# Masks of a small softmax: two full-array matmuls ahead of the scores, or twelve 32-column ones behind them

## The chip, the cores and the metric

The kernel runs on one core of one Trainium2 chip. The metric is the device time in microseconds of one execution, the median over several. The core has a matrix engine (TensorE, PE in the profile, its weight loads PEld), VectorE (DVE), ScalarE (ACT), GpSimd (POOL) and SyncE (SP), which issues most DMAs.

## The reference

The whole program is four layers, A B A B, each added to the residual stream `x` of 2048 tokens of width 640. The change concerns layer B, a recurrent memory transformer with 32 heads of width 128:

```python
mask = (idx[:, None] < M) | (idx[:, None] >= idx[None, :])   # M = 8, L = 40
for s in range(n_seg):                                       # 64 segments of 32 tokens
    h = jnp.concatenate([mem, xs], axis=1)                   # 8 + 32 rows
    q, k, v = (jnp.einsum('btd,dhe->bhte', h, W) for W in (Wq, Wk, Wv))
    scores = jnp.einsum('bhqe,bhke->bhqk', q, k) * scale
    scores = jnp.where(mask[None, None], scores, -1000000000.0)
    p = _softmax(scores, axis=-1)
    o = jnp.einsum('bhqk,bhke->bhqe', p, v)
    o = jnp.einsum('bhte,hed->btd', o, Wo)
    mem = o[:, :M, :].copy()
    outs.append(o[:, M:, :])
```

The eight memory rows see everything; the other 32 rows are causal. The memory of one segment comes out of the segment before, so the 64 steps of a layer form a chain.

## The kernel before, in words

Layer B (`layer_B`) runs 64 steps, twice in the program, 128 in all. The order of the instructions on TensorE, ScalarE, VectorE and GpSimd is the order in which the code issues them: every engine is wrapped in `_OrdNC`, which chains each instruction behind the one before on its engine. All profile lines of layer B read L101, the line of that wrapper, so groups are told apart by tile names.

A step `s` projects 32 columns, the 8 memory rows and the first 24 tokens of a segment, with 32-column tiles of the matrix engine, four side by side: K and Q for heads 0 to 15 (`b_Ka`, `b_Qa`) and for heads 16 to 31 (`b_Kb`, `b_Qb`). Each result is evacuated from PSUM to a bf16 tile `b_kq`, by ScalarE for Ka, Kb and Qb and by VectorE for Qa, and transposed back with four full-array matmuls (`transp4`: `b_TPak`, `b_TPaq`, `b_TPbk`, `b_TPbq`). VectorE copies the memory rows of each transpose into `QT[s]` and `KT[s]`, and ScalarE the 24 token rows into those of step `s + 1`.

The last 8 tokens of each segment (the tails) do not depend on the memory. They are projected for eight segments at a time in spare places of the chain (`tail_unit`, tile `b_tail`), go through DRAM, and are copied by GpSimd (`tails_copy`) into `KT[s]` and `QZ[s % 2]`. `QZ` holds the tail queries of head pairs: 8 columns of the even head, zeros, 8 columns of the odd head.

The scores are built in two PSUM tiles of rows of 40 keys. `SPa` has 8 such rows per partition: 4 for the tail queries and 4 for the 32 other queries of heads 0 to 15; `SPb` has 4, for heads 16 to 31. `mask_mm` writes the masks first, as identity times `mask12` over the full 128x128 array: 320 columns into `SPa` between the transposes `b_TPbk` and `b_TPbq`, and 160 into `SPb` behind `b_TPbq`. `scores` then adds 64 matmuls of 40 columns in 32-column tiles: 16 with `b_QT` (heads 0 to 15), 32 with `b_QZ` (16 weight columns each) and 16 with `b_QT` (heads 16 to 31).

`mask12` is zero outside a few columns: in the tail rows only keys 0 to 7 are masked anywhere, in the other rows only keys 0 to 31 (the order of keys in `KT` is tail, tokens, memory).

The softmax follows: negated row maxima (`b_negmax`) and their addition to `SPa` and `SPb` on VectorE, the exponential (`b_E`) on ScalarE, sums (`b_ssum`), reciprocals and the products `b_Px` on VectorE and `b_Pm` on GpSimd. Meanwhile TensorE does the V projections (`b_Va`, `b_Vb`) and 30 matmuls of `b_tail`. Then it transposes the probabilities (`p_transp`, tile `b_PTP`), does 10 more of `b_tail`, the products with V (`b_OTP`), the output projection (`b_OPS`, and `b_OPSd` for the tails of earlier steps), and extracts the new memory (`b_MT`), with which the next step's K and Q begin.

Most PSUM tiles of layer B rotate through five buffers (`ps_tile`); `b_tail` and `b_TPbq` share one of their own.

Of the kernel before, what the change touches and what calls it, by code (L numbers as in the profile page):

```python
# [18 lines left out]
F32 = mybir.dt.float32  # L19
BF16 = mybir.dt.bfloat16  # L20
# [521 lines left out]
def layer_B(nc, tc, C, W, x_src, xb_src, x_dst, mem0, B_Wv, B_Wo, nsteps=64, out_bf16=False, tag=""):  # L542
    SCB = 1.0 / math.sqrt(128.0)
    nc_raw = nc
    nc = _OrdNC(tc, nc_raw, engines=ORDER_ENGINES)
# [4 lines left out]
    with ExitStack() as ctx:  # L550
        def pool(name, bufs):
            return ctx.enter_context(tc.tile_pool(name=name, bufs=bufs, reuse_waits="tile"))
# [8 lines left out]
        st = pool("b_state", 1)  # L561
# [10 lines left out]
        def ps_tile(shape, dtype, name):  # L572
            return pp.tile(shape, dtype, name=name, tag="ps")
# [2 lines left out]
        Px = st.tile([128, 12, 32], BF16, name="b_Px")  # L576
        Pm = st.tile([128, 12, 32], BF16, name="b_Pm")
        mask12 = st.tile([128, 12, 40], BF16, name="b_mask12")
        QZ = [st.tile([128, 16, 24], BF16, name=f"b_QZ{i}") for i in range(2)]
        selm = st.tile([128, 2, 8], BF16, name="b_sel")  # L580
        HXz = st.tile([128, NCH, 1, 32], BF16, name="b_HXz")
        OTdef = [wk.tile([128, 32, 32], BF16, name=f"b_OTdef{i}") for i in range(2)]
# [1 line left out]
        def init_state():  # L584
# [7 lines left out]
            for i in range(2):  # L592
                nc.gpsimd.memset(QZ[i][:], 0.0)
            negs = wk.tile([128, 32], F32, name="b_negs", tag="PTa")
# [71 lines left out]
        def transp4(sb, name, tp=None):  # L666
            if tp is None:
                tp = ps_tile([128, 4, 128], BF16, name)
            for i in range(4):
                nc.tensor.transpose(tp[:, i, :], sb[:, 128 * i:128 * i + 128], C.identb[:])  # L670
            return tp
# [10 lines left out]
        def tails_load(s):  # L682
            tl = bx.tile([128, 2, 32, 8], BF16, name="b_tl", tag="tl")
            nc.sync.dma_start(tl[:].rearrange("p a h t -> p (a h t)"), QKd[s])
            return tl

        def tails_copy(s, tl):
            for e in range(2):
                nc.gpsimd.tensor_copy(QZ[s % 2][:, :, 16 * e:16 * e + 8], tl[:, 0, :, :].rearrange("p (x e) t -> p e x t", e=2)[:, e])
            nc.gpsimd.tensor_copy(KT[s][:, :, 0:8], tl[:, 1, :, :])  # L690

        def vtails_in(s):
# [96 lines left out]
        for (nm, b), sb in zip(jobs, sbs):  # L789
            tp = transp4(sb, "b_TP")  # L790
            scatter("dve" if nm == "K" else "act", tp, b, KT[0] if nm == "K" else QT[0], 8, 32, 8 if nm == "K" else 0)
        XO, XOd = init_state()
        tails_copy(0, tails_load(0))
        Vth = VH[-1] = w2.tile([128, 2, 512], BF16, name="b_Vth", tag="Vth")
        for k in range(8):
# [61 lines left out]
        for s in range(nsteps):  # L857
# [7 lines left out]
            if not last:  # L865
                alloc_seg(s + 1)
                tl = tails_load(s + 1)
# [3 lines left out]
            def x_scatter(tp, b, D_):  # L871
                if not last:
                    scatter("act", tp, b, D_[s + 1], 8, 32, 8 if D_ is KT else 0)
# [5 lines left out]

            GR = ((0, 8), (8, 12))  # L880

            def mask_mm(a):
                g0, g1 = GR[a]
                SP = ps_tile([128, g1 - g0, 40], F32, f"b_SP{a}")
                nc.tensor.matmul(SP[:].rearrange("p g k -> p (g k)"), lhsT=C.identb[:], rhs=mask12[:, g0:g1, :].rearrange("p g k -> p (g k)"),
                                 start=True, stop=False, skip_group_check=True)
                return SP

            def scores(SPs):
                for b in range(2):  # L890
                    for j in range(4):
                        for i in range(4):
                            h = 16 * b + 4 * j + i
                            nc.tensor.matmul(SPs[b][32 * i:32 * i + 32, j + 4 * (1 - b), :], lhsT=QT[s][:, h, :], rhs=KT[s][:, h, :],
                                             start=False, stop=True, tile_position=(0, 32 * i), skip_group_check=True)
                    if b == 0:
                        qz = QZ[s % 2][:].rearrange("p x c -> p (x c)")
                        for j in range(4):
                            for e in range(2):
                                for t4 in range(4):  # L900
                                    pr = 8 * (t4 // 2) + 2 * j + t4 % 2
                                    nc.tensor.matmul(SPs[0][32 * t4:32 * t4 + 16, j, :], lhsT=qz[:, 24 * pr + 8 * e:24 * pr + 8 * e + 16],
                                                     rhs=KT[s][:, 2 * pr + e, :],
                                                     start=False, stop=True, tile_position=(0, 32 * t4), skip_group_check=True)

            negmax = sm.tile([128, 12], F32, name="b_negmax", tag="negmax")
            ssum = sm.tile([128, 12], F32, name="b_ssum", tag="ssum")
# [2 lines left out]

            def soft_max(a, SP):
                nc.vector.tensor_reduce(out=negmax[:, slice(*GR[a])], in_=SP[:], axis=AX.X, op=ALU.max, negate=True)

            def soft_sub(a, SP):
                n_ = GR[a][1] - GR[a][0]
                nc.vector.tensor_tensor(out=SP[:], in0=SP[:], in1=negmax[:, slice(*GR[a])].unsqueeze(2).to_broadcast([128, n_, 40]), op=ALU.add)

# [45 lines left out]
            TPbk = transp4(kb, "b_TPbk")  # L963
            scatter("dve", TPbk, 1, KT[s], 0, 8, 32)
            x_scatter(TPbk, 1, KT)
            SPa = mask_mm(0)
            TPbq = transp4(qb, "b_TPbq", po.tile([128, 4, 128], BF16, name="b_TPbq", tag="tail"))
            scatter("dve", TPbq, 1, QT[s], 0, 8, 24)
            x_scatter(TPbq, 1, QT)
            SPb = mask_mm(1)  # L970
            scores((SPa, SPb))
            soft_max(0, SPa)
            soft_max(1, SPb)
# [10 lines left out]
            if not last:  # L984
                tails_copy(s + 1, tl)
# [55 lines left out]
            if not last:  # L1041
# [5 lines left out]
                for pi, (ca, cb) in enumerate(parts):  # L1047
                    mt = ps_tile([128, cb - ca, 8], F32, f"b_MT{pi}")
                    for c in range(ca, cb):
                        for q in range(4):  # L1050
                            o = 64 * c + 32 * (q % 2)
                            nc.tensor.matmul(mt[32 * q:32 * q + 32, c - ca, :], lhsT=msb[:, o:o + 32], rhs=selm[:, q // 2, :],
                                             start=True, stop=True, tile_position=(0, 32 * q), skip_group_check=True)
# [22 lines left out]
def full_kernel(tc, A_x, A_wq, A_wk, A_wv, A_wo, A_beta, B_x, B_mem0, B_Wq, B_Wk, B_Wv, B_Wo, B_seg_len, out, layers="ABAB"):  # L1076
    nc = tc.nc
    with ExitStack() as ctx:
# [15 lines left out]
        for li, L in enumerate(layers):  # L1094
            lastl = (li == nl - 1)
            if L == "A":
                first = li == 0

                def side(G, after):
                    load_B_resident(nc, WB, B_Wq, B_Wk, G, after)  # L1100
                    if G == 6:
                        keep_padded(nc, tc, WA, padded)

                layer_A(nc, tc, C, WA, xin if first else X, X, first, xb_dst=Xb,
                        load_w=lambda: load_A_weights(nc, WA, A_wq, A_wk, A_wv, A_wo, padded, stage),
                        side_loads=(side, A_beta) if first else None)
            else:
                layer_B(nc, tc, C, WB, X, Xb, xout if lastl else X, mem0, B_Wv, B_Wo, out_bf16=lastl, tag=str(li))
# [58 lines left out]
```

## Time and profile before

| what | value |
|---|---|
| median of 3 runs | 2805.99 us (2799.53 to 2806.8) |
| profiled execution | 2809.46 us, its span 2807.7 us |
| mean granted clock of TensorE | 0.984 |
| TensorE matmul busy | 2637.4 us, 94% of the span, 65416 records |
| TensorE weight loads busy | 1720.3 us, 61% |
| VectorE busy | 1688.6 us, 60% |
| ScalarE busy | 1589.9 us, 57% |
| mask matmuls of `b_SP` | 128 of 320 columns, mean 299 ns, and 128 of 160 columns, mean 233 ns |
| score matmuls with `b_QT` | 4096, mean 185 ns |
| score matmuls with `b_QZ` | 4096, mean 181 ns |

How to read it: a step of layer B takes some 14.9 us, so 128 steps make two thirds of the time. Matmuls are drawn from their start to a modelled end and overlap each other, so a mean of 185 ns says little of what one costs: what counts is how far apart the starts of neighbours are. Weight loads run beside matmuls.

### The profile page before, as it was taken

To read this page: it belongs to the slowest core of one execution; us is meant where nothing else is said; L and a number is where in the kernel's file an instruction comes from. 1 tells how busy PE (TensorE), PEld (TensorE's weight loads), DVE (VectorE), ACT (ScalarE), POOL (GpSimd) and SP (SyncE) were. 2 spreads that over 40 slices of the span, in tenths; PEclk is the share of its full clock that TensorE was granted. 3 is DMA by queue.
4 is the path that set the end of the run, shared out by engine and by line. 5 is a ranking of instruction groups with operands and counts; after the bars stand their busy time and mean duration, and the time that the engine had idled before them with its cause. 6 is when DMAs were issued, how large, how long until landed. Compare 5 with 4: busy or idle time off the path is not lost.

```text
span 2807.7 us, 146964 instructions
## 1 busy us (share of the span) xinstructions
PE 2637.4 (94%) x65416; PEld 1720.3 (61%) x65480; DVE 1688.6 (60%) x4553; ACT 1589.9 (57%) x3708; POOL 701.5 (25%) x1645
## 2 busy tenths in 40 slices
PE   5899988999999999999979999899999999999998
PEld 3555555666666666666645555556666666666665
DVE  6788864555555555545568888545555555555554
ACT  3778864555555555544448888445555555455443
POOL 3566651111111111111135666411111111111110
PEclk9999989999999999999989999899999999999999
DMA  6110143122122122111130111621111121111110
GB/s 213 65 44 30 30 165 104 41 45 45 41 44 44 41 47 46 39 42 31 29 112 21 58 48 37 218 55 40 42 41 39 42 43 40 42 41 36 39 27 20
DMA packets 322302, 156.36 MB, mean 56 GB/s; under 512 B 245761, under 2 KB 310401, under 8 KB 318593
## 3 DMA queue, kind: packets, MB, share of 16 engines
q1 hardware_dynamic: 320224, 136.47, 19.2%
q8 instruction: 512, 8.39, 1.3%
q10 hardware_dynamic: 1440, 10.49, 1.1%
q14 instruction: 126, 1.02, 0.1%
HBM read 95.15 MB, written 51.71 MB: 52 GB/s over the span
## 4 chain that ended last, share of the span: by engine, by line
PE 76%; ACT 8%; DVE 8%; issue 3%; DMA 3%; POOL 2%; SPq 0%; ACTq 0%; POOLq 0%; DVEq 0%
PE b_OPS L101 10%; PE b_tail L101 6%; PE b_Ka L101 5%; PE b_Qb L101 5%; PE b_Kb L101 5%; PE b_Qa L101 5%; PE b_Va L101 5%; PE b_Vb L101 5%; PE b_SP L101 4%; PE b_OTP L101 3%; DVE a_nm L369 3%; ACT a_PT L404 3%; PE b_PTP L101 3%; PE b_OPSd L101 3%; PE b_vtail L101 3%
## 5 line engine op out<-in xcount | busy, mean ns | idle before, releaser
L101 PEld LDWEIGHTS <-b_HX 128*32 128x32 bf16 x15360 | 435.9, 97 | 337.2 <-issue 15.8
L369 DVE TENSOR_REDUCE a_nm<-a_S 128x2 f32<-128x1024 f32 (+3 forms) x512 | 403.1, 808 | 70.0 <-PE a_T L401 58.1
L101 POOL TENSOR_TENSOR b_Pm<-b_E,b_rs 128x96 bf16<-128x96 bf16 x128 | 63.4, 495 | 1446.2 <-ACT b_Vth L101 1118.7
L404 ACT ACTIVATE a_PT<-a_T 128x1024 bf16<-128x1024 f32 (+1 forms) x384 | 342.3, 895 | 77.9 <-PE a_T L401 72.7
L101 PE MATMUL b_OPS<-b_wo,b_OTsb 128*32 128x320 bf16 x8192 | 309.7, 301 | 12.2 <-issue 9.9
L101 PEld LDWEIGHTS <-b_OTsb 128*32 128x32 bf16 x8192 | 202.1, 97 | 96.4 <-DVE b_OTsb L101 24.1
L406 POOL TENSOR_SCALAR_AFFINE_SELECT a_PT<-a_PT 128x256 bf16<-128x256 bf16 (+1 forms) x384 | 204.4, 534 | 196.1 <-ACT a_PT L404 195.4
L101 DVE CAST b_HX<-b_MT 128x8 bf16<-128x8 f32 x372 | 63.7, 172 | 280.4 <-PE b_MT L101 275.2
L101 ACT CAST b_msb<-b_OPS 128x64 bf16<-128x64 f32 x378 | 69.6, 257 | 239.5 <-PE b_OPS L101 239.5
L101 ACT CAST b_kq<-b_Kb 128x512 bf16<-128x512 f32 x128 | 74.9, 585 | 201.4 <-PE b_Kb L101 201.4
L101 DVE COPY b_KT<-b_TPak 128x128 bf16<-128x128 bf16 x128 | 28.8, 225 | 226.7 <-PE b_TPak L101 226.7
L101 PE MATMUL b_Va<-b_wv,b_HX 128*32 128x512 bf16 x2520 | 161.0, 380 | 0.0
L101 PE MATMUL b_Vb<-b_wv,b_HX 128*32 128x512 bf16 x2520 | 160.2, 379 | 0.0
L101 PEld LDWEIGHTS <-b_kq 128*128 128x128 bf16 x2080 | 116.8, 98 | 69.4 <-ACT b_kq L101 55.2
L101 PE MATMUL b_Ka<-b_wk,b_HX 128*32 128x512 bf16 x2520 | 159.3, 379 | 0.0
L101 PE MATMUL b_Qb<-b_wq,b_HX 128*32 128x512 bf16 x2520 | 159.2, 379 | 0.0
L101 PE MATMUL b_Kb<-b_wk,b_HX 128*32 128x512 bf16 x2520 | 159.2, 379 | 0.0
L101 PE MATMUL b_Qa<-b_wq,b_HX 128*32 128x512 bf16 x2520 | 159.2, 379 | 0.0
L101 DVE TENSOR_SCALAR b_kq<-b_Qa 128x512 bf16<-128x512 f32 x128 | 88.6, 692 | 116.7 <-PE b_Qa L101 113.7
L401 PE MATMUL a_T<-a_q,a_kT 32*128 32x512 bf16 (+3 forms) x1024 | 137.4, 305 | 19.5 <-DVE a_nm L369 12.9
L101 DVE CAST b_OTsb<-b_OTP 128x160 bf16<-128x160 f32 (+1 forms) x384 | 122.3, 374 | 39.3 <-PE b_OTP L101 39.3
L101 PE MATMUL b_vtail<-b_wv,b_TX 128*32 128x256 bf16 x2880 | 138.0, 271 | 7.9 <-issue 4.9
(195 smaller groups left out, 5777.3 us busy)
## 6 DMA issues: line engine op xcount, KB each, us to landing
b_QKd<-b_tu SPq DMA_DIRECT2D x128, 128.0 KB
b_tl<-b_QKd SPq DMA_DIRECT2D x128, 128.0 KB
b_wv<-in_B_Wv_dram SPq DMA_DIRECT2D x10, 1024.0 KB
b_wo<-in_B_Wo_dram SPq DMA_DIRECT2D x16, 640.0 KB
b_VTd<-b_vt SPq DMA_DIRECT2D x256, 32.0 KB
b_Vth<-b_VTd SPq DMA_DIRECT2D x512, 16.0 KB
b_XO<-xres SPq DMA_DIRECT2D x256, 30.0 KB
b_wk<-in_B_Wk_dram ACTq DMA_DIRECT2D x5, 1024.0 KB
```

Of the source, the lines that this page charges most:

```text
L101: r = f(*a, **k)
L369: nc.vector.tensor_reduce(out=nm[:, qc, 2 * pr:2 * pr + 2], in_=X[:, :, o:o + w_], axis=AX.X, op=ALU.max, negate=True)
L401: nc.tensor.matmul(Y[:, e, o:o + w_], lhsT=kT[rows, 128 * kc:128 * kc + 128], rhs=q2[rows, 128 * kc:512], start=True, stop=True, tile_posi ...
L404: nc.scalar.activation(out=PT[:, :, b:b + width], in_=Y[:, :, 0:width], func=ACT.Exp, scale=SC)
L406: nc.gpsimd.affine_select(out=dv, in_=dv, pattern=[[0, 2], [0, diag], [1, 128]], compare_op=ALU.is_ge, fill=0.0, base=0, channel_multiplie ...
```

## The change

`mask_mm` no longer opens the PSUM tiles. The first score matmul of each tile and quadrant does that (`start=(j == 0)`), and the masks are added behind the scores, in 32-column tiles of the array (weights: 32 columns of the identity), only in the columns where `mask12` is not zero: for `SPa` four matmuls of 4 x 8 columns (tail rows) and four of 4 x 32, for `SPb` four of 4 x 32. `SPb`'s masks stand behind its own scores.

The tail queries' matmuls wrote 16 of each 32 partitions; the other 16 were covered by the mask matmul. Now the matmul of the even head writes 32: `QZ` has 40 columns per head pair instead of 24, with 24 zeros in the middle.

```diff
-        QZ = [st.tile([128, 16, 24], BF16, name=f"b_QZ{i}") for i in range(2)]
+        QZ = [st.tile([128, 16, 40], BF16, name=f"b_QZ{i}") for i in range(2)]
...
-                nc.gpsimd.tensor_copy(QZ[s % 2][:, :, 16 * e:16 * e + 8], tl[:, 0, :, :].rearrange("p (x e) t -> p e x t", e=2)[:, e])
+                nc.gpsimd.tensor_copy(QZ[s % 2][:, :, 32 * e:32 * e + 8], tl[:, 0, :, :].rearrange("p (x e) t -> p e x t", e=2)[:, e])
...
-            def mask_mm(a):
+            def sp_tile(a):
                 g0, g1 = GR[a]
-                SP = ps_tile([128, g1 - g0, 40], F32, f"b_SP{a}")
-                nc.tensor.matmul(SP[:].rearrange("p g k -> p (g k)"), lhsT=C.identb[:], rhs=mask12[:, g0:g1, :].rearrange("p g k -> p (g k)"),
-                                 start=True, stop=False, skip_group_check=True)
-                return SP
+                return ps_tile([128, g1 - g0, 40], F32, f"b_SP{a}")
+
+            def mask_mm(SP, o0, o1, m0, w_):
+                for k in range(4):
+                    nc.tensor.matmul(SP[32 * k:32 * k + 32, o0:o1, 0:w_], lhsT=C.identb[:, 32 * k:32 * k + 32],
+                                     rhs=mask12[:, m0:m0 + o1 - o0, 0:w_],
+                                     start=False, stop=True, tile_position=(0, 32 * k), skip_group_check=True)
...
                             nc.tensor.matmul(SPs[b][32 * i:32 * i + 32, j + 4 * (1 - b), :], lhsT=QT[s][:, h, :], rhs=KT[s][:, h, :],
-                                             start=False, stop=True, tile_position=(0, 32 * i), skip_group_check=True)
+                                             start=(j == 0), stop=False, tile_position=(0, 32 * i), skip_group_check=True)
...
-                                    nc.tensor.matmul(SPs[0][32 * t4:32 * t4 + 16, j, :], lhsT=qz[:, 24 * pr + 8 * e:24 * pr + 8 * e + 16],
+                                    m_ = 16 if e else 32
+                                    nc.tensor.matmul(SPs[0][32 * t4:32 * t4 + m_, j, :], lhsT=qz[:, 40 * pr + 24 * e:40 * pr + 24 * e + m_],
                                                      rhs=KT[s][:, 2 * pr + e, :],
-                                                     start=False, stop=True, tile_position=(0, 32 * t4), skip_group_check=True)
+                                                     start=False, stop=False, tile_position=(0, 32 * t4), skip_group_check=True)
+                        mask_mm(SPs[0], 0, 4, 0, 8)
+                        mask_mm(SPs[0], 4, 8, 4, 32)
+                mask_mm(SPs[1], 0, 4, 4, 32)
...
-            SPa = mask_mm(0)
+            SPa = sp_tile(0)
             TPbq = transp4(qb, "b_TPbq", po.tile([128, 4, 128], BF16, name="b_TPbq", tag="tail"))
             scatter("dve", TPbq, 1, QT[s], 0, 8, 24)
             x_scatter(TPbq, 1, QT)
-            SPb = mask_mm(1)
+            SPb = sp_tile(1)
             scores((SPa, SPb))
```

## The prediction

> **What bounds the kernel now.** I read the profile page first, then the timeline of one B step, then the waits. The page's chain of waits is almost all TensorE:
>
> ```profile
> PE 76%; ACT 8%; DVE 8%; issue 3%; DMA 3%; POOL 2%; SPq 0%; ACTq 0%; POOLq 0%; DVEq 0%
> ```
>
> That share invites the reading "fewer matmul columns, less time". It is an average over unlike places, so I looked at the two spots where the change acts. The first is the timeline of one step from the last Q projection to the softmax (start, length, engine, operation):
>
> ```profile
> 1007.85 0.60 ACT L101 ACTIVATE b_kq<-b_Qb 128x512 bf16<-128x512 f32 x1 [0.50 <-PE b_Qb L101]
> ...
> 1008.29 0.10 PEld L101 LDWEIGHTS <-c_identb 128*128 128x128 bf16 x1
> ...
> 1008.35 0.30 PE L101 MATMUL b_SP<-b_mask,c_identb 128*128 128x320 bf16 x1
> ...
> 1008.50 0.23 PEld L101 LDWEIGHTS <-b_kq 128*128 128x128 bf16 x4
> ...
> 1008.73 0.23 PE L101 MATMUL b_SP<-b_mask,c_identb 128*128 128x160 bf16 x1
> ...
> 1008.90 0.28 PE L101 MATMUL b_SP<-b_KT,b_QT 128*32 128x40 bf16 x16
> ...
> 1009.01 0.41 PE L101 MATMUL b_SP<-b_KT,b_QZ 128*16 128x40 bf16 x32
> ...
> 1009.25 0.32 PE L101 MATMUL b_SP<-b_KT,b_QT 128*32 128x40 bf16 x16
> ...
> 1009.52 0.72 DVE L101 TENSOR_REDUCE b_negmax<-b_SP 128x8 f32<-128x320 f32 x2 [0.36 <-PE b_SP L101]
> ```
>
> Two things are to be seen. ScalarE's evacuation of Qb ends at 1007.848 + 0.597 = 1008.445, and the weight load for `b_TPbq` starts at 1008.496. In all 128 steps of the two B layers that load starts 50 to 52 ns after that evacuation ends: the four transposes wait for ScalarE, and the first mask matmul (148 ns from its start to theirs) stands inside this wait. And VectorE is idle until the scores of `SPa` are complete.
>
> The second spot is the next meeting of VectorE and TensorE, on the weight loads before `b_PTP`:
>
> ```profile
> 1012.32 0.27 PEld L101 LDWEIGHTS <-b_wk 128*128 128x128 bf16 x7
> 1012.72 0.11 PEld L101 LDWEIGHTS <-b_Px 128*128 128x128 bf16 x2
> 1012.92 0.11 PEld L101 LDWEIGHTS <-b_Pm 128*128 128x128 bf16 x2
> 1013.07 0.11 PEld L101 LDWEIGHTS <-b_Px 128*128 128x128 bf16 x2
> ```
>
> VectorE's two `b_Px` products end at 1012.662 and 1013.018, and the loads that need them start 54 ns later; the second distance is 52 to 54 ns in all 128 steps. TensorE has nothing to do at 1012.55, when the last of the thirty `b_tail` matmuls has streamed. The matmul rows hide this, since each is drawn some 180 ns or more long. So the cycle that sets a step is: Qb, its evacuation, `b_TPbq`, scores of `SPa`, softmax on VectorE and ScalarE, `b_PTP`. TensorE's work between `SPa` and `b_PTP` has slack.
>
> **The change part by part.** Nanoseconds per step, from the starts of single matmuls in this step; the spread over the steps is a few ns where none is given.
>
> *First mask matmul removed: 0.* Its cover is the evacuation. Without it `b_TPbq` could start 56 ns after the last `b_TPbk` matmul instead of 56 + 148, but the load still waits until 1008.496. If that were not a real wait, 148 ns would come free (a rival).
>
> *Second mask matmul removed: −67.* It stands between the last `b_TPbq` matmul and the first score, with no wait that ends later: 56 ns to it, then 163 to the scores. 163 is 67 for 160 columns (2.4 columns per ns, the pace at which 512-column matmuls in four tiles follow each other, 54 ns apart) plus 96 for going from the full array to 32-column tiles. That step stays: elsewhere it is 126 after 27 ns of columns (`b_tail` to `b_OTP`) and 152 after 53 (layer A). So 53 + 98 = 151 replaces 219. The scores' own inputs are ready: `b_QT` from `b_TPaq` ends at 1008.550, and the scores would start at 1008.83; the second half needs `b_QT` from `b_TPbq`, ending at 1009.158 plus 51, and would start at about 1009.27.
>
> *A separate semaphore instruction before the first score: 0.* In the built program the score's load now carries two waits, for the buffer's last writer (Kb, long past) and VectorE. Such an instruction already stands in the `b_tail` to `b_OTP` turn, which costs 99 beyond its columns, no more than turns without one.
>
> *Weight tiles of the tail queries 32 instead of 16 wide (16 of 32): 0.* The loads last 93 and 86 ns, but lie beside matmuls: rounds of four matmuls start every 25 ns both with `b_QT` (32 wide) and with `b_QZ` (16 wide).
> The Trainium skill, "TensorE: Matmul & The Clock Gate", section "LDWEIGHTS (loading the stationary operand)", makes a load cost its columns ÷ 1.2 ns, 13 ns more for each widened one; over four tiles side by side that would be an estimated 53 ns per step, 6.8 us in all. The equal rounds of 25 ns speak against paying it, since in them the load is hidden.
>
> *Eight mask matmuls ahead of `SPa`'s release: +104.* From about the 33rd score on, pairs of load and matmul start 8.3 ns apart, so eight add 67. The last one streams 128 columns where the last `b_QZ` streams 40: 88 ÷ 2.4 = 37 more before it is done. Writing runs of 8 or 32 into rows of 40 costs nothing extra: `b_PTP` does exactly that and its matmuls follow each other at 55 ns for 128 columns and 26 to 28 for 32, like contiguous ones.
>
> *Release of VectorE.* From the last `b_QZ` start to `b_negmax` it now takes 277; 314 with the longer matmul. The other bound is the nearest 128-column row, `b_TPbq` to its VectorE copy: 255. I take 314, because the same kind of matmul in the same place gives it; 255 would make the sum −22 instead of +37.
>
> *Second-half masks, +53, and the later start of Va: 0.* TensorE reaches `b_PTP` about −67 + 33 + 53 + 53 = 72 later, `b_PTP` itself waits 37 longer; in the step shown it waits 164 at the first load and longer in all. `SPb` is ready about 100 later than now, and VectorE takes it up only 0.41 us after `SPa`.
>
> *POOL and SP:* same instructions; two memsets per layer grow from 384 to 640 elements, in the prologue. The copies into `QZ` keep their size and count.
>
> Sum: −67 + 67 + 37 = **+37 ns per step, times 128 = +4.7 us**, 2814.2 us against the profiled execution (2809.46, its span 2807.7 plus 1.8) and **2810.7** against the median of 2805.99, which lies 3.5 below that execution; the shown runs spread over 7.3. With the 255 ns bound: −22 × 128 = −2.8, 2803.2. 0.3% is 8.4 us, about what a measurement of this kernel can tell from no change; both ends lie inside it.
>
> **The rivals.**
>
> *The dense run breaks up more often (slower).* In 57 of the 128 steps `b_negmax` starts later than the usual 277, by 128 ns on average and up to some 220, 7.3 us in all. In most of them TensorE's starts also show one hole among the last of the 64 scores, never before the 57th pair. No wait explains it; it looks as if a long run of such short instructions outruns something. The run grows from 64 to 76 pairs, and `SPa` completes after the 56th instead of the 48th. If every step lost the mean of 128, 71 more would cost 9.1 us: +13.8, **2819.8**; with 220 in each step +25.5, 2831.5. Against it: some late steps show no hole, so length need not be the cause. It decides over no change from about 29 more late steps (3.7 us).
>
> *`b_TPbq` moves up (faster).* If the load at 1008.496 only stood behind the 320 columns (133 ns), the step would gain 148 more: 37 − 148 = −111, −14.2 us, **2791.8**. For: 148 is not far above 133. Against: the constant 50 to 52 ns to the evacuation's end, while the distance to the mask matmul varies from 135 to 153.
>
> *Wide loads are paid.* If each of the 16 held up the row difference of 7 ns in a single file, 112 ns on the chain: +149 in all, 19.1 us, **2825.1**. The rounds of 25 ns speak against it. The skill's rule above is a milder form of this and would give 2817.5, within this rival's chance.
>
> *TensorE takes over before `b_PTP`.* If the slack is smaller than the profile shows, +72 counts instead of +37: 9.2 us, **2815.2**. It decides where the waits on `b_Px` vanish; the 52 to 54 ns in every step speak against it.
>
> *The change doesn't do what it says* is unlikely: the built order has 12 mask matmuls behind the scores and none ahead.
>
> **How the numbers follow.** Forecast with both bounds: 0.60, between 2803 and 2811 plus a few us of spread. Dense run: 0.22. `b_TPbq` moves up: 0.10. Wide loads: 0.04. TensorE takes over: 0.04. Faster by over 0.3%: 0.10, from the second rival alone. Slower by over 0.3%: 0.22 + 0.04 + 0.04 = 0.30. Within: 0.60. The range runs from 2798, the lower bound less the spread of runs, to 2824, which takes in most of the dense run's cases; outside are the second rival, the wide loads in single file and every step at 220.
>
> **What would show it.** Right: `b_TPbq` loads still 50 to 52 ns after the Qb evacuation; 151 ns from the last `b_TPbq` matmul to the first score; mask matmuls 8.3 ns apart; `b_negmax` some 314 after the last of them; `b_PTP` still 53 after `b_Px`. Wrong: the load earlier than the evacuation allows, scores in rounds longer than 33 ns, holes ahead of `SPa`'s last mask matmul, or more late `b_negmax` than 57.

## The result, and the profile after

The changed kernel takes **2824.77 us** (median of 6 runs, 2818.03 to 2827.35) beside 2804.94 for the kernel before (6 runs, 2799.53 to 2807.38): ratio 1.0073, 95% interval 1.0062 to 1.0084. It is slower by 19.8 us. The forecast was 2810.7, less than 0.3% above before, and its range ended at 2824: the result lies just above it. The profiled execution of the change took 2827.12 us, its span 2825.4 at a clock of 0.982; against the profiled one of before (2807.7) that is 17.7 us of span to explain.

First the place of the change. The timeline of one undisturbed step after it (start, length, engine, operation; the idle time before it and who ended that in brackets):

```profile
1029.47 0.60 ACT L101 ACTIVATE b_kq<-b_Qb 128x512 bf16<-128x512 f32 x1 [0.50 <-PE b_Qb L101]
...
1030.12 0.23 PEld L101 LDWEIGHTS <-b_kq 128*128 128x128 bf16 x4 [0.16 <-ACT b_kq L101]
1030.12 0.40 PE L101 MATMUL b_TPbq<-c_identb,b_kq 128*128 128x128 bf16 x4
...
1030.45 0.28 PE L101 MATMUL b_SP<-b_KT,b_QT 128*32 128x40 bf16 x16
...
1030.56 0.41 PE L101 MATMUL b_SP<-b_KT,b_QZ 128*32 128x40 bf16 x32
...
1030.80 0.28 PE L101 MATMUL b_SP<-b_mask,c_identb 128*32 128x32 bf16 x8
...
1030.90 0.29 PE L101 MATMUL b_SP<-b_KT,b_QT 128*32 128x40 bf16 x16
...
1031.01 0.25 PE L101 MATMUL b_SP<-b_mask,c_identb 128*32 128x128 bf16 x4
...
1031.14 0.72 DVE L101 TENSOR_REDUCE b_negmax<-b_SP 128x8 f32<-128x320 f32 x2 [0.35 <-PE b_SP L101]
```

Both full-array masks are gone, `b_TPbq` is still released by ScalarE's evacuation, and the twelve small masks stand where the diff puts them. From the start of `b_TPbq` to `b_negmax` it is 1017 ns here, and 1017 in such a step of before (15th percentile over the steps; 1016 after). So in an undisturbed step the change moves the chain by nothing. But fewer steps are undisturbed: `b_negmax` comes more than 30 ns later than this in 52 of the 128 steps before and in 68 after. The rest of the loss lies further down.

At the second meeting, before `b_PTP`, nothing has changed either. In the step ahead of the one shown VectorE's products end at 1018.33 + 0.78 = 1019.11, and the load that needs the second starts right behind that:

```profile
1018.33 0.78 DVE L101 TENSOR_TENSOR b_Px<-b_E,b_rs 128x256 bf16<-128x256 bf16 x2
...
1018.81 0.11 PEld L101 LDWEIGHTS <-b_Px 128*128 128x128 bf16 x2
...
1019.17 0.11 PEld L101 LDWEIGHTS <-b_Px 128*128 128x128 bf16 x2
```

The page's chain of waits doesn't tell the difference: it is TensorE as before, one per cent more.

```profile
PE 77%; ACT 8%; DVE 7%; issue 3%; DMA 2%; POOL 1%; SPq 0%; ACTq 0%; DVEq 0%; POOLq 0%
```

The waits of TensorE that nothing in the profile releases ("issue": waited in us, times, longest us), first before, then after:

```profile
PE b_OPS L101 <- issue: 9.9, 18, 1.0
...
PE b_vtail L101 <- issue: 4.9, 10, 0.7
PE b_OPSd L101 <- issue: 4.2, 5, 1.2
PE b_MT L101 <- issue: 4.1, 10, 0.9
```

```profile
PE b_OPS L101 <- issue: 16.2, 25, 1.5
...
PE b_OPSd L101 <- issue: 7.3, 7, 4.0
...
PE b_vtail L101 <- issue: 6.5, 13, 0.9
```

These are idle times of TensorE inside the output projection, which begins some 5.5 us behind the masks, and they grow. The timeline of one such place after, and the same stretch of another step without a hole:

```profile
714.62 1.53 PE L101 MATMUL b_OPS<-b_wo,b_OTsb 128*32 128x320 bf16 x40
...
717.66 0.46 PE L101 MATMUL b_OPS<-b_wo,b_OTsb 128*32 128x320 bf16 x8 [1.51 <-issue]
...
718.22 0.55 ACT L101 CAST b_msb<-b_OPS 128x64 bf16<-128x64 f32 x3 [3.47 <-PE b_OPS L101]
```

```profile
730.43 2.36 PE L101 MATMUL b_OPS<-b_wo,b_OTsb 128*32 128x320 bf16 x64
```

64 matmuls take 2.36 us when they run through; here the last 8 start 1.5 us late with their inputs long ready, and ScalarE's `b_msb`, the new memory, waits behind them. This is on the chain of every step: `b_msb`, `b_MT`, `b_HX`, the next `b_Ka`.

Where does the 17.7 us go? Means over 126 steps, from the starts of single instructions, in ns:

| stretch of the step | before | after | difference |
|---|---|---|---|
| start of `b_TPbq` to `b_negmax` | 1074 | 1099 | +25 |
| `b_negmax` to the last `b_PTP` | 3713 | 3721 | +8 |
| first to last `b_OPS` (median 2058, 2059) | 2186 | 2293 | +106 |
| all else | 8054 | 8059 | +5 |
| whole step | 15027 | 15172 | +145 |

145 × 126 = 18.3 us, the whole loss. 106 of it are the holes in `b_OPS`; 25 come from the steps in which `b_negmax` is late. The undisturbed value of neither stretch moves.

**What the holes are.** The program has 131104 TensorE instructions before and 133792 after, and the page lists a queue that carries TensorE's instructions (packets, MB, share of the DMA engines), before and after:

```profile
q8 instruction: 512, 8.39, 1.3%
```

```profile
q8 instruction: 522, 8.55, 1.3%
```

131104 ÷ 512 = 256.06 and 133792 ÷ 522 = 256.3: a packet is a block of 256 instructions. Counted from the program's start, the first instruction behind a hole is nearly always number 194 or 195 of its block: 66 of the 86 holes over 0.35 us from `b_OPS` to `b_MT` after, 48 of 69 before, and no other number more than twice. The one above is number 25795 = 100 × 256 + 195. TensorE had started the load before it at 715.842, a packet landed at 716.080, and TensorE went on at 717.663. I read that as some 62 instructions taken in ahead of time, so that what is late is the next block. In those 66 holes (48 before) the median from the landing to the next start is 1.40 us (1.43). The packet takes 1.13 us on average, and in layer B it starts 1.04 us (median; 0.93 before) after TensorE has come within 64 instructions of the end of the block two before. By this reading it takes some 3.5 us (the sum of the three) from there until the new block can be used, so TensorE must stop when it uses up 256 instructions in less; no two packets start less than 3.29 us apart. From the first `b_OTP` load on, 256 instructions are used up in 2.84 us (medians). And from the first score to the start of the last `b_OPS` matmul an undisturbed step takes 7.85 us with 577 instructions before, and 7.91 us with 601 after: 3.48 and 3.37 us per block, just about as fast as blocks come.

The Trainium skill, "Runtime: NRT & Kernel Launch", section "Instruction fetch mechanics", has the blocks of 256 instructions, which agrees, but gives TensorE room for 2048 instructions and says that the fetch is hidden, because dispatch is slower than the fill. This trace disagrees: in 94 steps of equal length the holes at block edges sum to 31.4 us before and 50.0 after.

### The profile page after: what moved, and what is told of

Its sections match the earlier page's. It is cut to its first block, busy times and chain, and to the rows that moved or that the text cites. A ratio compares the mean times of both kernels' runs of the same rounds, so it can differ in the third digit from the quotient of the medians.

```text
span 2825.4 us, 149652 instructions
## 1 busy us (share of the span) xinstructions
PE 2652.7 (94%) x66696; PEld 1723.8 (61%) x66760; DVE 1688.6 (60%) x4553; ACT 1595.3 (56%) x3708; POOL 702.4 (25%) x1645
## 3 DMA queue, kind: packets, MB, share of 16 engines
q14 instruction: 125, 1.02, 0.1%
## 4 chain that ended last, share of the span: by engine, by line
PE 77%; ACT 8%; DVE 7%; issue 3%; DMA 2%; POOL 1%; SPq 0%; ACTq 0%; DVEq 0%; POOLq 0%
PE b_OPS L101 10%; PE b_tail L101 6%; PE b_Ka L101 5%; PE b_Kb L101 5%; PE b_Qb L101 5%; PE b_Qa L101 5%; PE b_Va L101 5%; PE b_Vb L101 5%; PE b_SP L101 4%; PE b_OTP L101 3%; ACT a_PT L404 3%; DVE a_nm L369 3%; PE b_vtail L101 3%; PE b_OPSd L101 3%; PE b_PTP L101 3%
## 5 line engine op out<-in xcount | busy, mean ns | idle before, releaser
L101 PE MATMUL b_OPS<-b_wo,b_OTsb 128*32 128x320 bf16 x8192 | 315.6, 301 | 19.6 <-issue 16.2
L401 PE MATMUL a_T<-a_q,a_kT 32*128 32x512 bf16 (+3 forms) x1024 | 138.0, 306 | 16.9 <-DVE a_nm L369 10.4
```

Of the source, the lines that this page charges most:

```text
L101: r = f(*a, **k)
L401: nc.tensor.matmul(Y[:, e, o:o + w_], lhsT=kT[rows, 128 * kc:128 * kc + 128], rhs=q2[rows, 128 * kc:512], start=True, stop=True, tile_posi ...
```

## The experiments

The theories: **supply**, the number of TensorE instructions per step sets the loss, wherever they stand; **late release**, the masks behind the scores delay `b_negmax` in more steps (the first rival of the prediction); **chain**, the eight masks cost their length ahead of the release. All kernels were timed beside the kernel before on the same chip; "late" is the sum by which steps go over the kernel's own usual time from `b_TPbq` to `b_negmax` by more than 30 ns; "holes" is the excess at block edges in the 94 equal steps. Late and holes come from one profiled execution each. Before was traced once, so its 7.1 and 31.4 stand beside traces from other chips.

| kernel | instr. per step | ratio to before [95%] | late, us | holes, us |
|---|---|---|---|---|
| before | 869 | 1 | 7.1 | 31.4 |
| after | 890 | 1.0073 [1.0062, 1.0084] | 10.4 | 50.0 |
| after_again | 890 | 1.0052 [1.0040, 1.0064] | 9.5 | 34.1 |
| after_c | 890 | 1.0054 [1.0040, 1.0068] | 8.7 | 47.1 |
| after_d | 890 | 1.0045 [1.0030, 1.0060] | 9.8 | 31.1 |
| pad10 | 889 | 1.0012 [1.0002, 1.0021] | 6.5 | 27.6 |
| pad10_b | 889 | 1.0010 [0.9999, 1.0022] | 5.9 | 33.5 |
| pad10_scores | 889 | 1.0026 [1.0016, 1.0035] | 7.1 | 30.5 |
| pad15 | 899 | 1.0032 [1.0020, 1.0044] | 6.6 | 25.9 |
| pad20 | 909 | 1.0073 [1.0060, 1.0086] | 6.2 | 42.9 |
| long4 | 877 | 1.0026 [1.0017, 1.0036] | 5.9 | 24.1 |
| before_less10 | 849 | 0.9988 [0.9976, 1.0000] | 5.0 | 26.2 |
| before_less10_b | 849 | 0.9983 [0.9970, 0.9996] | 5.3 | 25.7 |
| after_less10 | 870 | 1.0021 [1.0010, 1.0031] | 9.0 | 31.7 |
| after_less20 | 850 | 1.0014 [1.0005, 1.0022] | 9.3 | 23.4 |
| spa_unmasked | 890 | 1.0032 [1.0020, 1.0044] | 8.1 | 38.9 |
| masks_ahead | 871 | 0.9985 [0.9974, 0.9995] | 6.9 | 22.8 |
| masks_ahead_less10 | 851 | 0.9960 [0.9947, 0.9974] | 6.9 | 32.8 |

The same changed kernel shows 31 to 50 us of holes on different chips, so a single trace tells where the holes are, and only the ratios what a kernel costs.

**More instructions, away from the scores.** Pairs of weight load and 8-column matmul ahead of `b_Va`, where TensorE has slack; and four pairs of 512 columns, many columns in few instructions:

```diff
-        def thin_mm(cols_ap, Wt, b, name):
+        def thin_mm(cols_ap, Wt, b, name, pad=0, pad_w=8):
             ps = ps_tile([128, 512], F32, name)
+            for k in range(pad):
+                j = k % 4
+                nc.tensor.matmul(ps[32 * j:32 * j + 32, 0:pad_w], lhsT=cols_ap[:, 0, :], rhs=Wt[:, 0, 512 * (4 * b + j):512 * (4 * b + j) + pad_w],
+                                 start=True, stop=True, tile_position=(0, 32 * j), skip_group_check=True)
...
-            Va = thin_mm(cols, W.wv, 0, "b_Va")
+            Va = thin_mm(cols, W.wv, 0, "b_Va", pad=10, pad_w=8)   # pad15: 15, pad20: 20, long4: pad=4, pad_w=512
```

pad10: 

> The kernel before, with ten extra pairs of weight load and 8-column matmul per step, written into Va's PSUM tile ahead of its real first matmul, which overwrites them. Theory S (supply): TensorE's instructions reach it in blocks of 256, and from the scores to the output projection a step uses them about as fast as they come, so an instruction added there costs 5.7 ns although TensorE has slack at that place: 20 x 5.7 x 126 steps = +14 us, as holes without a wait in b_OPS; bounds +5 and +33 (13.3 ns each, the shortest distance of two blocks over 256). Theory D (dense scores and a longer mask chain): nothing in this kernel touches scores or masks, 0. Theory L (TensorE late at b_PTP): 83 ns of TensorE time in the slack, 0 if the slack holds, +10 at most.

pad20: 

> The kernel before with twenty pairs in Va's tile, twice as many as in pad10 (which gave +3.5 us). S: the more instructions a block's worth of time has to hold, the more edges stall: +7 us if linear, up to +20. L (TensorE late at b_PTP): 166 ns of TensorE time, 0 to +5, since 213 ns with few instructions gave +7.

pad15: 

> The kernel before with fifteen such pairs ahead of Va, 899 instructions a step. Ten cost 3 us, twenty 20. If the supply has a knee just above the count of pad10 and the change, fifteen cost 10 to 15 us; if the cost grows only well past the change's count, 5 us or less.

long4: 

> The kernel before, with four extra pairs of 512 columns at the same place: 213 ns more TensorE time in the slack ahead of b_PTP, but 8 instructions instead of 20. S: +5.7 us, bounds 0 and +13. L: if later V projections are what costs, 213 ns is nearly three times the 72 of the change, +27 us. D: 0.

pad10_b, beside the change on one chip: 

> The ten pairs in Va's tile again, now on the same chip as the changed kernel. S: as many instructions per step as the change (889 against 890), none of them on the chain: +4 to +12 us over the kernel before, and the changed kernel some 3 us (its late b_negmax) above that. If the masks' place matters beyond that, the changed kernel stays 10 us above this one.

Ten pairs cost 3.4 to 3.5 us (2801.34 beside 2797.82, 2807.55 beside 2804.16), fifteen 8.0 (2801.80 beside 2793.77), twenty 20.2 (2814.91 beside 2794.67), on four chips in all. So instructions that do nothing cost time in a place with slack, by these runs more than in proportion, and twenty of these pairs cost as much as the whole change did. Some 3 us of that come about because they use up the slack: the last `b_PTP` moves by 25 ns on average. Ten pairs, which bring the step to the change's number of instructions, cost less than the 5 us that the supply theory asked for at the least. On the one chip where pad10_b and the change both ran they cost 3.4 us of the change's 18.0: there, number alone isn't the cause. long4 gives the slack itself: its 213 ns of columns move the first `b_PTP` by 47 ns (median after `b_negmax` 3205 to 3252), so 166 ns lie free, the 164 of the prediction. The last `b_PTP`, with which the chain goes on, does not move in the median and by 22 ns on average, 2.8 us of long4's 6.8 (2804.59 beside 2797.82). Its holes are no longer than before's, and what makes the other 4 us isn't shown.

**Fewer instructions.** Ten of the thirty `b_tail` matmuls ahead of `b_PTP` left out (twenty in after_less20); a part of the tail projections is then not computed.

```diff
-                for c in range(NCH):
+                nch = NCH - dict(short).get(i, 0)
+                for c in range(nch):
...
-                tail_unit(work[0], work[1], 0, 6)
+                tail_unit(work[0], work[1], 0, 6, short=((0, 4), (1, 4), (2, 2)))
```

after_less10: 

> The changed kernel with ten of the thirty b_tail pairs ahead of b_PTP left out in every step (part of the tail projections is not computed): 20 instructions fewer, almost the count of the kernel before, in a place where TensorE waits for b_Px anyway. S: the holes in b_OPS fall back, 12 to 16 us less than the changed kernel, about +3 to +6 over the kernel before, which is the chain's share. D: no difference to the changed kernel, +20. L: 290 ns of TensorE time less ahead of b_PTP, so the changed kernel's loss would also go, wholly.

before_less10: 

> The kernel before with the same ten b_tail pairs left out. S: the kernel before has 27 us of such holes itself, so it gets faster, by 7 to 14 us. D and L: 0, since b_PTP waits for b_Px in every step.

before_less10_b: 

> The kernel before without the ten b_tail pairs, for the comparison with masks_ahead_less10 on the same chip: -3 to -4 us against the kernel before, as in the first comparison.

after_less20: 

> The changed kernel with twenty of the thirty b_tail matmuls ahead of b_PTP left out (part of the tail projections is not computed): 850 instructions a step, as many as the kernel before with ten left out (849), which ran at 0.998 to 0.999 of before. If the whole loss of the change is TensorE's instruction supply: -2 to -6 us against before, block-edge holes down to 26 us or less in the 94 steps. If something else in the change costs, half of its loss stays: +3 to +6 us as with ten left out, with few holes.

Taking ten pairs from before gains 0.12 to 0.17%, 3.6 to 3.8 us, about half of the least that the supply theory asked for. On one chip twenty taken from the change bring it from 1.0045 to 1.0014. That leaves it above before, at 19 instructions per step fewer than before, and, across chips, 0.26 to 0.31% above before_less10 with one instruction more. At 870 instructions it is 0.21% above before with 869. So some 0.2 to 0.3%, 6 to 9 us, do not go with the number of instructions in a step. What stays in the trace of after_less20 is the late release: 9.3 us of it against 5.0 and 5.3, while its holes (23.4) are below both.

**The place, and the masks themselves.** pad10_scores puts ten pairs where the change has its twelve masks, without touching what `SPa`'s release waits for:

```diff
+            def zero_mm(SP, n):
+                for k in range(n):
+                    nc.tensor.matmul(SP[32 * (k % 4):32 * (k % 4) + 32, 0, 32:40], lhsT=C.identb[:, 32 * (k % 4):32 * (k % 4) + 32],
+                                     rhs=mask12[:, 4, 32:40],
+                                     start=False, stop=True, tile_position=(0, 32 * (k % 4)), skip_group_check=True)
...
+                        zero_mm(SPs[1], 8)
+                zero_mm(SPs[1], 2)
```

> The kernel before with ten added pairs of weight load and matmul of 8 columns (identity times eight columns of the mask that are all zero, added to SPb), eight right behind the last score of SPa's tail rows, two behind SPb's scores: the places of the change's twelve masks, but nothing that SPa's release waits for, and 889 instructions a step like pad10. If the place of instructions beside the dense run of scores is what makes the change dearer than pad10: +10 to +15 us against before, with more and longer holes at block edges in b_OPS than pad10 (more than 35 us in the 94 steps of equal length). If only their number counts: about +3 us as pad10, holes 28 to 34 us, and the rest of the change's loss is then in what it does to SPa's release. SPb's scores start 67 to 83 ns later in both.

spa_unmasked is the changed kernel without the eight masks of `SPa` (`SPa` stays unmasked), with eight pairs ahead of `b_Va` in their stead:

```diff
-                        mask_mm(SPs[0], 0, 4, 0, 8)
-                        mask_mm(SPs[0], 4, 8, 4, 32)
...
-            Va = thin_mm(cols, W.wv, 0, "b_Va")
+            Va = thin_mm(cols, W.wv, 0, "b_Va", pad=8, pad_w=8)
```

> The changed kernel without the eight mask matmuls of SPa (its scores stay unmasked), but with eight pairs of 8 columns in Va's tile instead: the same number of instructions. Chain: SPa is complete some 67 ns earlier and its last matmul is shorter by 88 columns, which the changed kernel's trace shows to cost nothing: -67 to -104 ns x 126 = -8 to -13 us against the changed kernel. S, if the place of an instruction does not matter: the same -8 to -13 and no more; if instructions ahead of SPa cost more than those behind it, more than that.

after_again: 

> The changed kernel again, beside the other kernels of this call. S (block supply, with the prices that the first four runs gave: 20 instructions in TensorE's slack cost 3.5 us in the one kernel and 3.7 in the other, and the chain's own share is 3 to 5): +9 to +10 us over the kernel before, if instructions cost the same wherever they stand between the scores and b_OTP; +20 if the ones ahead of SPa cost more.

after_c: 

> The changed kernel on the same chip, for the comparison with pad10_b: +14 to +20 us over the kernel before, as in the two earlier comparisons.

after_d: 

> The changed kernel once more, as the yardstick for the other three on this chip: +15 us (+14.5 to +19.8 so far), block-edge holes 34 to 50 us in the 94 steps. If it falls below +10 here, the chip counts as much as the change, and pad15 and pad10_scores are read against it and not against the earlier chips.

On one chip pad10_scores costs 6.1 us (2799.88 beside 2793.77) and the change 10.0 (2803.72), at 889 and 890 instructions and with equal holes of 30.5 and 31.1. What differs in the traces is the late release, 7.1 and 9.8 us. Over all kernels it falls into two groups. Where no mask stands behind `SPa`'s scores and `SPb`'s, it is 5.0 to 7.1 us (11 traces, whatever the number of instructions from 849 to 909); with all twelve there, 8.7 to 10.4 (6 traces, from 850 to 890); with `SPb`'s four alone, 8.1. The means are 6.31 and 9.45: **+3.1 us, which goes with the masks behind the scores and not with the number**. Two other parts of the change go with it as well and were not taken out by themselves: the separate semaphore instruction ahead of the first score, and score matmuls that open the tiles. All kernels of the second group and spa_unmasked have both; none of the 11 has either. Taking `SPa`'s masks off the chain gains 0.20% (1.0052 to 1.0032 on one chip): `b_negmax` comes 79 ns earlier on average (1092 to 1013, × 128 = 10 us). The ratio gives 5.6 us of that; in the trace `b_PTP` ends 7 ns and `b_OPS` 26 ns later on average, relative to what they follow, and take back 33 of the 79.

A late step of the change, to be held against the one shown at the top:

```profile
1014.40 0.40 PE L101 MATMUL b_TPbq<-c_identb,b_kq 128*128 128x128 bf16 x4
...
1015.08 0.28 PE L101 MATMUL b_SP<-b_mask,c_identb 128*32 128x32 bf16 x8
...
1015.17 0.48 PE L101 MATMUL b_SP<-b_KT,b_QT 128*32 128x40 bf16 x16
...
1015.61 0.72 DVE L101 TENSOR_REDUCE b_negmax<-b_SP 128x8 f32<-128x320 f32 x2 [0.56 <-PE b_SP L101]
```

Up to `SPa`'s masks both steps run alike (0.68 us from `b_TPbq`). Then 16 scores take 0.48 us instead of 0.29, a hole with no wait (1015.217 to 1015.387), and `b_negmax` starts 0.53 us after the first mask instead of 0.34, though the last mask of `SPa` had started before the hole, at 1015.136. In all late steps of before and after, everything up to the start of `SPa`'s last matmul runs as in undisturbed ones, and the delay comes behind it. In 45 of the 52 late steps before, and 59 of the 68 after, TensorE has such a hole; counted from the first score, the first pair of load and matmul that comes late is the 61st to 63rd (median) in all 18 traces, whether `SPa`'s last matmul is the 48th or the 56th. These holes are not at block edges. What makes them I could not tell.

**A version without either cost.** masks_ahead trims the masks to their non-zero columns as the change does, but leaves them on the full array and puts all three matmuls between `b_TPbk` and `b_TPbq`, in the wait for ScalarE (`QZ` as in the change):

```diff
-            SPa = mask_mm(0)
-            TPbq = transp4(qb, "b_TPbq", po.tile([128, 4, 128], BF16, name="b_TPbq", tag="tail"))
+            SPa = ps_tile([128, 8, 40], F32, "b_SP0")
+            SPb = po.tile([128, 4, 40], F32, name="b_SP1", tag="tail")
+            mask_mm(SPa, 0, 4, 0, 8, True)
+            mask_mm(SPa, 4, 8, 4, 32, False)
+            mask_mm(SPb, 0, 4, 4, 32, True)
+            TPbq = transp4(qb, "b_TPbq")
...
-            SPb = mask_mm(1)
```

> A third version: the masks only in the columns where they are not zero, as in the change, but full-array and ahead of the scores, three matmuls (32, 128 and 128 columns) all between b_TPbk and b_TPbq, where TensorE waits for Qb's evacuation anyway; SPb takes the buffer of b_TPbq and b_TPbq the one of SPb. Two instructions more than the kernel before instead of 20. S and the chain: the 67 ns of the second mask go from the chain, the three matmuls (25 + 55 + 55 ns) fit into the 148 ns of the first: -67 x 126 = -8.4 us, 0.997. If the chain through SPa were not what sets the step: 0.

masks_ahead_less10, the same with ten `b_tail` matmuls left out: 

> The third version (masks ahead of the scores, trimmed, three matmuls) without ten of the thirty b_tail pairs. masks_ahead alone gained 4 us where 67 ns x 126 = 8.4 had been taken off the chain. S: the missing half was eaten by the instruction supply; with 20 instructions fewer the whole 8.4 shows against the kernel before with the same pairs left out. If the 67 ns are simply worth less: 4 us again.

It beats both kernels: 2788.52 beside 2794.67 on the chip on which the change took 2809.67. Its timeline:

```profile
1000.62 0.30 PE L101 MATMUL b_SP<-b_mask,c_identb 128*128 128x32 bf16 x3
1000.77 0.40 PE L101 MATMUL b_TPbq<-c_identb,b_kq 128*128 128x128 bf16 x4
...
1001.49 0.28 PE L101 MATMUL b_SP<-b_KT,b_QT 128*32 128x40 bf16 x16
...
1001.72 0.72 DVE L101 TENSOR_REDUCE b_negmax<-b_SP 128x8 f32<-128x320 f32 x2 [0.29 <-PE b_SP L101]
```

`b_negmax` comes 950 ns after `b_TPbq`, 67 to 69 earlier than before in the usual step: the second mask is off the chain and nothing has taken its place. 69 × 128 = 8.8 us were to be had; the ratio gives 4.2 [1.4, 7.3], the difference of the medians is 6.2. That the supply ate the rest is not shown: with ten pairs less it gains 0.23% on before_less10_b, the same size (intervals of ±0.13% each).

The two kernels of this chip in which `b_negmax` comes equally early in the usual step (948 ns in both) show what late release leaves out. spa_unmasked has 19 instructions more than masks_ahead and takes 13.3 us more (2801.80 beside 2788.52). In their traces `b_negmax` is 9 ns later on average, but from the last `b_PTP` to the last `b_OPS` it takes 96 ns more, 12 us in 126 steps, most of it in `b_OPS` (holes of 38.9 and 22.8 us). That is more than ten pairs ahead of `b_Va` cost on other chips; pad10 did not run on this one, and pad10_scores only on the chip where the holes stayed short, so whether place or chip makes the holes longer isn't separated.

## Why the prediction was wrong

- *First mask removed: 0.* Right. The load for `b_TPbq` still starts 50 to 52 ns after the evacuation's end in all steps, and the rival in which it moves up fell.
- *Second mask removed: −67.* Right: `b_TPbq` to the first score went from 396 to 327. In masks_ahead, where nothing takes the mask's place, it shows as time (4 to 6 of 8.8 us).
- *The separate semaphore instruction: 0.* Right for the chain: masks_ahead has no such instruction, and the same 327 to its first score.
- *Wide `QZ` loads: 0.* Right: the span of the `b_QZ` matmuls is 230 before, 234 after, 4 ns where that rival asked for 112.
- *Eight masks ahead of the release: +67.* Right: the last starts 67 after the last `b_QZ`, 8.3 apart.
- *128 columns instead of 40: +37.* **Mis-sized.** From the last mask to `b_negmax` it is 272 to 275 in usual steps, where it was 276 to 278 from the last `b_QZ`: −3. That lies between the bounds (255 and 314), and I took the wrong end. With it the chain's sum is −67 + 67 − 3 = −3 ns, 0.4 us, which is what undisturbed steps show (1017 to 1016).
- *Second-half masks and the later start of Va: 0.* Right for their time: the second `b_Px` load ahead of `b_PTP` still comes 51 to 54 ns after its product in 125 of 128 steps, and 166 ns were free. **But this is the step that failed:** costed by columns and starts alone, 12 mask pairs for 2 were free wherever TensorE had slack. They are also 21 more instructions per step that have to be fetched, and a slack in columns doesn't cover that: ten pairs, the same number, cost 3.4 to 6.1 us (pad10, pad10_scores), and 106 of the 145 ns that a step lost lie in `b_OPS`, most of them in holes at the edges of instruction blocks. The sum had no term for it, although the page of before showed the queue of 512 packets and the unexplained waits in `b_OPS`.
- *The rival of the dense run* was right in part. `b_negmax` is late in more steps, as its sign of being wrong said, but the term is 3.1 us rather than 9, and it is only part of the loss. That its 2819.8, and the 2825.1 of the wide loads, came near the result is luck: most of the loss came from holes in `b_OPS`, which neither has. *TensorE takes over ahead of `b_PTP`*: 8 ns per step, 1 us.

So the change's 10 to 20 us are, as far as runs show: some 3 us of late releases, 3.4 to 6.1 us for the number of instructions (pad10, pad10_scores), and, on the chips where the change cost most, longer holes at block edges than pads of the same number make: on one chip 47.1 us against 33.5, with 14.6 us between the two kernels. The first two nearly make up the 10 us of the one chip and less than half of the 19.8 of the first result. Why the same number gives longer holes elsewhere stays open, as do the other 3 to 6 of the 6 to 9 us that are left at equal numbers (their intervals are ±0.1% each).

## What to carry to other kernels

Count instructions as well as columns: where TensorE uses 256 instructions in less than some 3.5 us, as it did here, twelve tiny matmuls for two long ones were no saving, even in a place with slack. The sign is waits by "issue" in places with no dependency, always at the same instruction number within a block of 256; the packets of the instruction queue in the page give the number of blocks. Of the complete versions here the fastest puts the shortened operation into a wait that exists anyway, in almost as few instructions as before: masks_ahead.

## What the runs showed of the hardware that I had not expected

- TensorE is supplied with instructions in blocks of 256 with no more than about two blocks ahead: a packet starts 63 to 355 instructions before the first of its block runs, by this reading, and at the holes a new block was used 1.4 us (median) after it had landed.
- In layer B a packet of instructions starts 0.93 us (before) and 1.04 us (after, medians) after TensorE has come within 64 instructions of the end of the block two before. Traffic of the other queues in the 0.3 us behind that point makes no clear difference: 0.93 and 1.02 us with none, 0.86 and 1.07 with three or more of the 16 DMA engines busy.
- VectorE's release behind the scores was about the same for 40 and for 128 columns in the last matmul (276 to 278, 272 to 275 ns from its start in undisturbed steps).
- A dense run of pairs of load and matmul breaks in many steps near its 62nd pair, in every kernel of this case, without a wait that the profile shows; what breaks it is not known.
